# The second layer's inner weight sums and output additions of one batch: from GpSimd to VectorE

## The chip, the cores and the metric

The kernel runs on one core of one Trainium2 chip. The metric is the time of one execution on the device in microseconds (us), and where several executions are given, their median. Of the kernel before there are three: 904.57, 904.01 and 902.47 us, median 904.01. One more execution, of 905.66 us, was recorded by the hardware profiler, and all durations below come from that one. The engines are called PE (TensorE, the matmuls; PEld is its loading of weights), DVE (VectorE), ACT (ScalarE), POOL (GpSimd) and SP (SyncE, which here issues nearly all DMAs).

## The reference

Four batches of 768 tokens go through an attention block in which a query sees only the keys of its own cluster, and then through a feed-forward block of two layers. Only the latter matters here:

```python
def _moe_ref(x, w_in, w_out) -> np.ndarray:
    h = x @ w_in                                   # (3072, 512) @ (512, 2048)
    g = h * (1.0 / (1.0 + np.exp(-1.702 * h)))
    return (g @ w_out).astype(np.float32)          # (3072, 2048) @ (2048, 512)
```

## The kernel before, in words

After all the attention, the kernel runs the two layers for one batch after the other (the loop `for b in range(B)`, line 992). Both layers save matmuls by a scheme of Strassen's kind: a product of 2 x 2 blocks is made with seven block products instead of eight, and pays for it with additions of blocks before and after. The first layer (`first7`, line 843) does so once, in eight steps of seven products. The second layer does so twice, one level inside the other: seven outer products (the loop `for k in range(7)`, line 1044, in the order `ORDER = (1, 2, 3, 6, 5, 7, 4)`, line 751; called k = 0 to 6 here), and each of them is made by `second49` (line 886) from seven inner products.

Around these 49 products there are four kinds of additions, and the question is who makes them:

- The inner sums of the activations (`sums_t`, line 818): for each k four sums of 128x768, here called t3, t2, t1 and t4 in the order in which they are made, t2 and t1 depending on the one before. VectorE makes them one set ahead: during set k it makes those of k+1, two at the first, one at the second and one at the third call of `extra` in `second49`. The inner products 6, 5, 7 and 4 need t2, t1, t3 and t4. TensorE takes the products in the order 1, 2, 6, 5, 7, 3, 4, so t2 is needed first.
- The inner sums of the weights (three of 128x512, s2, s1 and s4, written by `keep_w`, line 770): the same for all batches. They are made once, in the first batch, and stored to DRAM (`kept_w`); later batches load them (`load_sums`, line 786). Those of k = 0 to 4 are made by GpSimd during the first batch's first layer, those of k = 5 and 6 during its second layer, right into the tile `Wz` from which TensorE reads them. The pool of `Wz` has two buffers, so the tile of k+2 takes that of k, and the call stands after `second49(k)`, that is after sets k = 3 and k = 4.
- The additions of an inner product into its block: 128x192, of a PSUM bank and an SBUF tile (`add`, line 841), by VectorE; y11, y12 and y22 are three quarters of the block `y`. Copies out of PSUM are ScalarE's. There are six PSUM banks, and a set takes three, so each bank comes round again two sets later.
- The additions of the finished block `y` into the output's quarters `Y[11]` to `Y[22]`, 128x768 each, at the end of `second49`: for k = 3, 4 and 5 (products 6, 5 and 7 of `ORDER`) two of them. GpSimd makes them, but in the last batch VectorE makes those of k = 4 and 5.

While VectorE is at k = 5 and 6 it also makes the sums of the next batch's x (`sums_x`, line 623, eight operations of 128x384), which the next first layer needs from its second product on; they and others are handed out by `extra`, which calls `more`. Each engine runs its instructions strictly in the order in which the program issues them. On every engine this order is the one written in the code, so an operation that is put on VectorE stands in line in front of everything that the code issues to VectorE after it. All element-wise sums go through one helper, `sums`, so line 594 stands for all of them in the profile and they are told apart by tile and shape.

Of the kernel before, what the change touches and what calls it, by code (L numbers as in the profile page):

```python
# [38 lines left out]
def fast(  # L39
# [26 lines left out]
    nc = tc.nc  # L66

    B, H, S, D = q.shape
# [523 lines left out]
    def sums(engine, todo):  # L592
        for o, a, op, b in todo:
            engine.tensor_tensor(out=o, in0=a, in1=b, op=(  # L594
                ALU.add if op == "+" else ALU.subtract))
# [157 lines left out]
    def W_of(i):  # L753

        def w(row, col):
            return lambda fq, m: w_out[
                :, row * FB + fq * FQ:row * FB + (fq + 1) * FQ,
                col * DN + m * P:col * DN + (m + 1) * P]

        def z(n):  # L760
            return lambda fq, m: Z_of[n][:, fq * FQ:(fq + 1) * FQ,
                                         m * P:(m + 1) * P]
        return {1: w(0, 0), 2: w(1, 0), 3: z(4), 4: w(1, 1), 5: z(1),
                6: z(2), 7: w(0, 1)}[i]
# [2 lines left out]
        a = W_of(i)  # L767
        sums(nc.vector, ((a(0, 1), a(0, 0), "-", a(0, 1)),))

    def keep_w(k, o):  # L770

        a = W_of(ORDER[k])
        s2, s1, s4 = o
        for i, (o, x, op, z) in enumerate((
                (s2, a(1, 1), "-", a(0, 1)), (s1, s2, "+", a(0, 0)),
                (s4, a(1, 0), "-", s2))):
            sums(nc.gpsimd, ((o, x, op, z),))
            nc.sync.dma_start(out=kept_w[k, i], in_=o)

    def spare_y():  # L780
# [3 lines left out]
    W = {}  # L784

    def load_sums(k, made=False):
        W[k] = ws.tile([P, 3, FQ, P], FP32, name="Wz")
        if made:
            keep_w(k, [W[k][:, i] for i in range(3)])
            return  # L790
        for i in range(3):
            nc.sync.dma_start(out=W[k][:, i], in_=kept_w[k, i])

    def G_of(i):

        k, h = {1: (0, 0), 7: (0, 1), 3: (1, 1), 2: (1, 0), 6: (0, 0),
                5: (1, 1), 4: (1, 0)}[i]
        return lambda fq, q: G[:, k * FB + fq * FQ:k * FB + (fq + 1) * FQ, h,
                               q * QT:(q + 1) * QT]
# [7 lines left out]
    def temps(k):  # L807

        return dict(zip((3, 2, 1, 4), (
            (tile_y(11), E[0], E[1], E[2]),  # L810
            (tile_y(12), tile_x(2), tile_x(3), tile_x(4)),
            (tile_y(21), E[0], E[1], E[2]),
            (tile_x(2), tile_x(3), tile_x(4), E[0]),
            (G_of(5)(0, 1), E[1], E[2], E[0]),
            (G_of(7)(0, 1), tile_x(3), E[1], E[2]),
            (G_of(4)(0, 1), E[0], E[1], E[2]))[k]))
# [23 lines left out]
    def add(o, p, a):  # L840
        nc.vector.tensor_tensor(out=o, in0=p, in1=a, op=ALU.add)  # L841
# [44 lines left out]
    def second49(k, extra, last):  # L886

        i = ORDER[k]
        a, g, t, w = W_of(i), G_of(i), temps(k), W.pop(k)
        A = {1: a(0, 0), 2: a(1, 0), 3: w[:, 2], 4: a(1, 1), 5: w[:, 1],  # L890
             6: w[:, 0], 7: a(0, 1)}
        M = {1: g(0, 0), 2: g(1, 0), 3: g(1, 1), 4: t[4], 5: t[1], 6: t[2],
             7: t[3]}

        def bank_b():
            return ps_b.tile([P, 512], FP32, name="b")[:, 0:QT]

        def product(ps, n, start):
            for f in range(FQ):
                nc.tensor.matmul(out=ps, lhsT=A[n][:, f], rhs=M[n][:, f],  # L900
                                 start=start and f == 0,
                                 stop=(f == FQ - 1), skip_group_check=True)

        y = Y[22] if i == 1 else ep.tile([P, 2, HALF], FP32, name="y")
        y11, y12, y21, y22 = (y[:, m, q * QT:(q + 1) * QT]
                              for m in range(2) for q in range(2))
        p5 = ep.tile([P, QT], FP32, name="p5")
        x = bank_b()
        product(x, 1, True)
        nc.scalar.copy(y11, x)  # L910
        z = bank_b()
        product(z, 2, True)
        add(y11, z, y11)
        extra(0)
        product(x, 6, False)
        nc.scalar.copy(y12, x)
        v = bank_b()
        product(v, 5, True)
        nc.scalar.copy(p5, v)
        product(x, 7, False)  # L920
        nc.scalar.copy(y22, x)
        add(y22, y22, p5)
        extra(1)
        product(v, 3, False)
        add(y12, v, y12)
        if i == 4:
            c = Y[21]
            add(c[:, 0], y[:, 0], c[:, 0])
            add(c[:, 1, QT:], y22, c[:, 1, QT:])
            extra(2)  # L930
        product(x, 4, False)
        if i == 4:
            add(c[:, 1, 0:QT], x, c[:, 1, 0:QT])
            return
        nc.scalar.copy(y21, x)
        extra(2)
        pool = nc.vector if last and i in (5, 7) else nc.gpsimd
        sums(pool, {1: (),
                    2: ((Y[11], y, "+", Y[22]),),
                    3: ((Y[12], y, "+", Y[22]),),  # L940
                    6: ((Y[12], y, "+", Y[12]), (Y[21], y, "+", Y[22])),
                    5: ((Y[12], y, "+", Y[12]), (Y[22], y, "+", Y[21])),
                    7: ((Y[22], y, "+", Y[22]), (Y[21], y, "+", Y[21]))}[i])
# [42 lines left out]
    def do(steps, n):  # L986
        for _ in range(n):
            next(steps, None)
# [3 lines left out]
    for b in range(B):  # L992
        for f in range(FB):
            first7(b, f, *XT)
            sums_w(b * FB + f + 2)
            if f:
                after7(f - 1)
            do(pend, 1)
            if b == 0 and f < 3:
                for n in range(3 * f, min(3 * f + 3, FB)):  # L1000
                    sums_z((nc.gpsimd, nc.vector, nc.vector)[n % 3], n)
            if b == 0 and f in (3, 4):
                for i in ORDER[0:4] if f == 3 else ORDER[4:]:
                    turn_w(i)
            if b == 0 and f >= 3:
                for k in {3: (0,), 4: (1, 2), 5: (3,), 6: (4,), 7: ()}[f]:
                    keep_w(k, spare_y())
                if 5 <= f < 7:
                    load_sums(f - 5)
        after7(FB - 1)  # L1010
        if b < B - 1:
            for h in range(2):
                for hp in range(HP):
                    x = xT_of[b + 1, h, hp] = xp.tile([P, HALF], FP32,
                                                      name="x")
                    nc.sync.dma_start(out=x, in_=kept[b, h, hp])
            made = sums_x(b + 1)
        else:
            made = iter(())

        def stores(b, *todo, **how):
            for n in todo:
                store(b, n, **how)
                yield

        def tail():
            store(b, 22)
            yield
            store(b, 21, q=slice(1, 2))
            store(b, 21, q=slice(0, 1), queues=(), turned=slice(0, 1))  # L1030
            yield

        def chain(*todo):
            for steps in todo:
                yield from steps

        def sums_of_x():
            for XT[:] in made:
                yield

        x_steps = sums_of_x()
        final = b == B - 1

        for k in range(7):
            nxt = sums_t(k + 1) if k < 6 else iter(())
            more = {1: sums_G(6), 2: sums_G(5), 3: sums_G(4),
                    4: stores(b, 11), 5: stores(b, 12) if final else x_steps,
                    6: tail() if final else x_steps}.get(k, iter(()))
            if b == B - 1 and k < 2:
                test(k)  # L1050
            if (b, k) == (B - 1, 6):
                is_bad = nc.values_load(bad[0:1, 0:1], min_val=0, max_val=1)

            def extra(at):
                do(nxt, (2, 1, 1)[at])
                do(more, ((1, 0, 1) if final else (0, 4, 4))[at] if k == 6
                   else (0, 0, 4)[at] if k == 2 else (0, 2, 2)[at])

            second49(k, extra, final)
            if k < 5:  # L1060
                load_sums(k + 2, b == 0 and k > 2)
            elif b < B - 1:
                load_sums(k - 5)
        pend = () if final else stores(b, 12, 22, 21)
        if final:
            store(b, 21, q=slice(0, 1), turned=slice(1, 2),
                  queues=(nc.sync, nc.scalar))
# [439 lines left out]
```

## Time and profile before

| | us |
|---|---|
| median of the three runs (lowest, highest) | 904.01 (902.47, 904.57) |
| the profiled execution | 905.66 |
| its span, first to last instruction | 903.8 |
| GpSimd's 128x512 inner weight sums in the first batch's second layer, six | 1.27 to 1.98 each |
| GpSimd's 128x768 output additions from 456 to 484 us | 2.39 each (mean of 6) |
| VectorE's 128x768 output additions in the last batch, four | 0.94 to 0.95 each |
| matmul of the second layer, 128x192 | 0.326 |

The mean granted TensorE clock is 0.995. The first batch's second layer begins at 415.27 us and the second batch's at 555.59. A time in a timeline row is the start from the beginning of the span, followed by the duration; brackets at the end of a row give the idle time before it and who ended it. VectorE's rows overlap a little at their ends, so that the distance between two starts is some 0.08 us less than a duration where the next operation doesn't need the result.

In the first batch, the sets begin on TensorE at 433.76 (k = 2), 442.86 (k = 3), 451.96 (k = 4), 461.06 (k = 5) and 471.27 (k = 6), and the next first layer at 481.59. The chain of waits that ended last goes through TensorE alone nearly everywhere; between 454.79 and 484.54 us it runs mostly over VectorE's sums. At 480.85 this chain also names a load of `Wz` that lands at 483.88, just ahead of a VectorE sum at 483.94. That sum reads x and no `Wz`, and VectorE had worked without a break until then.

### The profile page before, as it was taken

Reading aid. Unit: us, or ns where it says so; the run is one execution under the profiler, and the core shown is the slowest. Engines: PE = TensorE matmul, PEld = TensorE weight load, DVE = VectorE, ACT = ScalarE, POOL = GpSimd, SP = SyncE. Lnnn points to the kernel's source line nnn. Section 1 sums busy time; section 2 is a strip of 40 time slices with the busy share of each in tenths; the row PEclk is TensorE's granted clock in tenths of the full one; section 3 lists DMA queues with packets and bytes.
Section 4 is the critical chain, followed back from the end, with each engine's and each line's share of the span. In section 5 each row is a group of like instructions: output and inputs, shape, how many; then the busy total and the mean of one; then the engine's idle time right before and its main releaser. Section 6 shows DMA issues by size and latency. Waiting matters only on the chain.

```text
span 903.8 us, 17747 instructions
## 1 busy us (share of the span) xinstructions
PE 885.9 (98%) x6712; PEld 581.7 (64%) x6712; DVE 728.1 (81%) x1170; ACT 365.0 (40%) x816; POOL 499.2 (55%) x469
## 2 busy tenths in 40 slices
PE   8999999999999999999999999999999999999994
PEld 3444444444454445558996557997557997557994
DVE  3999989999898997998998557797556797556894
ACT  3677767776777764222111222112222112222110
POOL 5899999999999998693274211242221242220230
PEclk9999999999999999999999999999999999999998
DMA  9466556666664210036213102332102322200323
GB/s 181 113 123 116 103 119 134 139 140 137 138 134 112 85 43 18 9 127 214 70 54 122 36 1 71 105 86 83 42 1 70 106 74 90 47 1 1 105 73 71
DMA packets 177565, 78.97 MB, mean 87 GB/s; under 512 B 154440, under 2 KB 160704, under 8 KB 177472
## 3 DMA queue, kind: packets, MB, share of 16 engines
q1 hardware_dynamic: 176912, 77.63, 35.3%
q8 instruction: 55, 0.90, 0.4%
q14 instruction: 38, 0.31, 0.1%
q10 hardware_dynamic: 560, 0.13, 0.1%
HBM read 61.03 MB, written 16.70 MB: 86 GB/s over the span
## 4 chain that ended last, share of the span: by engine, by line
PE 88%; DVE 6%; issue 2%; POOL 2%; DMA 1%; SPq 0%; ACT 0%; DVEq 0%; POOLq 0%
PE b L850 32%; PE b L900 23%; PE s L468 13%; PE o L533 12%; PE m L550 3%; PE s L491 3%; DVE G L594 2%; POOL sum L517 2%; DVE E L594 1%; PE m L344 1%; DVE Tx L594 1%; DMA in<-in_k_dram 1%; DVE y L841 0%; PE o L292 0%; DMA Wz<-kept_w 0%
## 5 line engine op out<-in xcount | busy, mean ns | idle before, releaser
L517 POOL TENSOR_TENSOR sum<-sum,A 128x384 f32<-128x384 f32 x252 | 265.9, 1091 | 26.7 <-ACT A L499 16.0
L841 DVE TENSOR_TENSOR G<-b,G 128x384 f32<-128x384 f32 x224 | 123.2, 557 | 98.9 <-PE b L850 89.3
L499 ACT ACTIVATE A<-s 128x768 f32<-128x768 f32 x192 | 146.2, 808 | 91.8 <-PE s L491 73.0
L594 POOL TENSOR_TENSOR Y<-y,Y 128x768 f32<-128x768 f32 x28 | 69.2, 2487 | 174.9 <-DVE y L841 151.0
L855 ACT ACTIVATE G<-G 128x384 f32<-128x384 f32 x128 | 66.4, 523 | 199.0 <-DVE G L841 197.7
L468 PE MATMUL s<-T,T 64*64 64x384 f32 x1536 | 143.0, 487 | 0.7 <-ACT A L499 0.7
L533 PE MATMUL o<-A,inv 64*64 64x384 f32 x1536 | 141.4, 483 | 0.0
L594 POOL TENSOR_TENSOR W<-w_in 128x256 f32<-128x256 f32 x32 | 23.6, 738 | 163.8 <-PE b L850 163.5
L594 DVE TENSOR_TENSOR G<-G 128x768 f32<-128x768 f32 (+1 forms) x92 | 102.3, 1136 | 0.0
L468 PEld LDWEIGHTS s<-T,T 64*64 64x64 f32 x1536 | 55.2, 132 | 69.9 <-ACT A L499 36.4
L850 PE MATMUL b<-Tx,w_in 128*128 128x384 f32 x256 | 93.0, 486 | 0.0
L850 PE MATMUL b<-x,W 128*128 128x384 f32 x256 | 93.0, 486 | 0.0
L850 PE MATMUL b<-x,w_in 128*128 128x384 f32 x256 | 88.6, 486 | 0.0
L533 PEld LDWEIGHTS o<-A,inv 64*64 64x64 f32 x1536 | 59.1, 133 | 37.9 <-issue 32.8
L850 PEld LDWEIGHTS b<-x,W 128*128 128x128 f32 x256 | 48.6, 190 | 33.9
L850 PEld LDWEIGHTS b<-Tx,w_in 128*128 128x128 f32 x256 | 48.6, 190 | 33.9
L850 PEld LDWEIGHTS b<-x,w_in 128*128 128x128 f32 x256 | 48.5, 190 | 33.5 <-issue 0.6
L900 PE MATMUL b<-G,w_out 128*128 128x192 f32 x320 | 55.9, 326 | 0.0
L900 PEld LDWEIGHTS b<-G,w_out 128*128 128x128 f32 x320 | 52.7, 190 | 1.1
L900 PE MATMUL b<-E,Wz 128*128 128x192 f32 x288 | 51.5, 328 | 1.4 <-DVE E L594 1.4
L900 PEld LDWEIGHTS b<-E,Wz 128*128 128x128 f32 x288 | 47.1, 190 | 3.4 <-POOL Wz L594 1.3
L850 PE MATMUL b<-Tx,W 128*128 128x384 f32 x128 | 46.6, 487 | 1.5 <-DVE Tx L594 1.5
(165 smaller groups left out, 1366.9 us busy)
## 6 DMA issues: line engine op xcount, KB each, us to landing
Wz<-kept_w SPq DMA_DIRECT2D x78, 256.0 KB
raw<-in_moe_w_in_dram SPq DMA_DIRECT2D x16, 512.0 KB
raw<-in_moe_w_out_dram SPq DMA_DIRECT2D x16, 512.0 KB
inv<-in_v_dram SPq DMA_DIRECT2D x16, 384.0 KB
in<-in_q_dram SPq DMA_DIRECT2D x60, 96.0 KB
in<-in_k_dram SPq DMA_DIRECT2D x60, 96.0 KB
kept<-x SPq DMA_DIRECT2D x24, 192.0 KB
x<-kept SPq DMA_DIRECT2D x24, 192.0 KB
```

Of the source, the lines that this page charges most:

```text
L344: nc.tensor.matmul(out=ps[r:r + SQ, w * NJ * SQ:(w + 1) * NJ * SQ] .rearrange("p (j t) -> p j t", t=SQ), lhsT=cT[:, p % HP].rearrange("p a ...
L468: nc.tensor.matmul(out=ps[c:c + D, a, 0:HALF], lhsT=T[p, 1][rows, kt * P + c:kt * P + c + D], rhs=T[p, 0][rows, h * HALF:(h + 1) * HALF], ...
L491: nc.tensor.matmul(out=s_of[u][c:c + D, a, :], lhsT=rows_of[1, p % 2][rows, kt * P + c:kt * P + c + D], rhs=rows_of[0, p % 2][rows, h * HA ...
L499: nc.scalar.activation(out=A_of[u], in_=s_of.pop(u), func=AF.Exp, scale=SCALE)
L517: nc.gpsimd.tensor_tensor(out=sum_of[g][:, a], in0=(A_of[u - 1] if kt == 1 else sum_of[g])[:, a], in1=A_of[u][:, a], op=ALU.add)
L533: nc.tensor.matmul(out=o_of[g][a * D:(a + 1) * D, r, 0:HALF], lhsT=v_in[p][rows, a, kt, :], rhs=A[rows, a, :], start=(kt == 0), stop=(kt = ...
L550: nc.tensor.matmul(out=ps[a * D:(a + 1) * D, 0:HALF], lhsT=twos, rhs=sm[:, a, :], start=(i == 0), stop=(i == len(parts) - 1))
L594: engine.tensor_tensor(out=o, in0=a, in1=b, op=(ALU.add if op == "+" else ALU.subtract))
L841: nc.vector.tensor_tensor(out=o, in0=p, in1=a, op=ALU.add)
L850: nc.tensor.matmul(out=ps[:, 0:HALF], lhsT=a[:, c], rhs=x(c), start=(c == 0), stop=(c == 1))
L855: nc.scalar.activation(out=g, in_=g, func=AF.Gelu_apprx_sigmoid, scale=2.0)
L900: nc.tensor.matmul(out=ps, lhsT=A[n][:, f], rhs=M[n][:, f], start=start and f == 0, stop=(f == FQ - 1), skip_group_check=True)
```

## The change

`keep_w` gets the engine as an argument. The two sets of inner weight sums that are made in the first batch's second layer (k = 5 and k = 6, three sums each) are issued to VectorE instead of GpSimd; those made earlier stay on GpSimd. And the four output additions of k = 4 and k = 5 in the first batch are issued to VectorE, as in the last batch. In both kernels they stand at the same places in the program: the output additions at the end of `second49`, the weight sums after it.

```diff
-    def keep_w(k, o):
+    def keep_w(k, o, engine=nc.gpsimd):
 
         a = W_of(ORDER[k])
         s2, s1, s4 = o
         for i, (o, x, op, z) in enumerate((
                 (s2, a(1, 1), "-", a(0, 1)), (s1, s2, "+", a(0, 0)),
                 (s4, a(1, 0), "-", s2))):
-            sums(nc.gpsimd, ((o, x, op, z),))
+            sums(engine, ((o, x, op, z),))
             nc.sync.dma_start(out=kept_w[k, i], in_=o)
...
         W[k] = ws.tile([P, 3, FQ, P], FP32, name="Wz")
         if made:
-            keep_w(k, [W[k][:, i] for i in range(3)])
+            keep_w(k, [W[k][:, i] for i in range(3)], nc.vector)
             return
...
-            second49(k, extra, final)
+            second49(k, extra, b in (0, B - 1))
             if k < 5:
                 load_sums(k + 2, b == 0 and k > 2)
```

On VectorE this adds three `Wz` sums after set k = 3, two output additions and three `Wz` sums after set k = 4, and two output additions after set k = 5; ten instructions. GpSimd loses the same ten. The instruction lists of the other engines are the same in both kernels, with the stores of the weight sums waiting for VectorE instead of GpSimd.

## The prediction

> **What bounds the kernel now.** I read the page first, then the timeline of TensorE through the first batch's second layer beside the same stretch of the second batch, then VectorE's and GpSimd's there. The page says that TensorE is the bound of the whole:
>
> ```profile
> PE 885.9 (98%) x6712; PEld 581.7 (64%) x6712; DVE 728.1 (81%) x1170; ACT 365.0 (40%) x816; POOL 499.2 (55%) x469
> PE 88%; DVE 6%; issue 2%; POOL 2%; DMA 1%; SPq 0%; ACT 0%; DVEq 0%; POOLq 0%
> ```
>
> An edit on VectorE or GpSimd can only bring time where TensorE waits for them. Busy times of two stretches, each from the first product of a second layer to the second product of the next batch's first layer:
>
> ```profile
> 415.27:484.54 69.27, 66.36 (x398) 64.14 (x396) 63.55 (x76) 12.70 (x38) 30.13 (x14) 1.00 0.33 112
> 555.59:620.84 65.25, 65.25 (x397) 64.43 (x396) 59.23 (x79) 11.40 (x36) 19.20 (x8) 1.00 0.29 91
> ```
>
> The columns are the stretch, its length, then PE, PEld, DVE, ACT and POOL busy. The same work takes 69.27 us in the first batch and 65.25, without a gap, in the second: 4.02 us of TensorE waiting, the most that this change can give. TensorE's timeline has the waits; a product of 8 matmuls takes 1.30, one of 4 in the first layer 1.29:
>
> ```profile
> 461.06 2.76 PE L900 MATMUL b<-G,w_out 128*128 128x192 f32 x16
> 463.78 1.54 PE L900 MATMUL b<-Tx,Wz 128*128 128x192 f32 x8
> 465.99 1.54 PE L900 MATMUL b<-E,Wz 128*128 128x192 f32 x8 [0.67 <-DVE E L594]
> ...
> 471.27 2.76 PE L900 MATMUL b<-G,w_out 128*128 128x192 f32 x16
> 474.06 1.57 PE L900 MATMUL b<-E,Wz 128*128 128x192 f32 x8
> 476.32 1.54 PE L900 MATMUL b<-E,Wz 128*128 128x192 f32 x8 [0.69 <-DVE E L594]
> ...
> 484.54 1.56 PE L850 MATMUL b<-Tx,W 128*128 128x384 f32 x4 [1.49 <-DVE Tx L594]
> ```
>
> Starts against what a gapless row would give: product 6 of set k=5 is 0.12 late (463.78 for 463.66), its product 5 0.91 (465.99 for 465.08), products 6 and 5 of k=6 0.19 and 0.96, the second product of the first layer 1.66 or so; together about 4. Each waits for a VectorE sum, but for 474.06, which begins 0.05 after GpSimd's first inner weight sum of k=6 ended (472.03 + 1.98). VectorE has no idle time in this stretch, so the question is why it is late:
>
> ```profile
> 461.73 1.91 DVE L594 TENSOR_TENSOR Tx<-G 128x768 f32<-128x768 f32 x1
> 468.09 2.30 DVE L594 TENSOR_TENSOR G<-G 128x768 f32<-128x768 f32 x1
> 470.43 2.45 DVE L594 TENSOR_TENSOR E<-G 128x768 f32<-128x768 f32 x1
> 474.15 2.02 DVE L594 TENSOR_TENSOR E<-G,E 128x768 f32<-128x768 f32 x1
> 479.24 4.24 DVE L594 TENSOR_TENSOR x<-x 128x384 f32<-128x384 f32 x2
> ```
> ```profile
> 458.90 1.98 POOL L594 TENSOR_TENSOR Wz<-w_out 128x512 f32<-128x512 f32 x1
> 460.96 1.86 POOL L594 TENSOR_TENSOR Wz<-Wz,w_out 128x512 f32<-128x512 f32 x1
> 462.79 1.98 POOL L594 TENSOR_TENSOR Wz<-w_out,Wz 128x512 f32<-128x512 f32 x1
> 467.18 4.88 POOL L594 TENSOR_TENSOR Y<-y,Y 128x768 f32<-128x768 f32 x2 [2.42 <-DVE y L841]
> 478.59 4.47 POOL L594 TENSOR_TENSOR Y<-y,Y 128x768 f32<-128x768 f32 x2 [1.30 <-DVE y L841]
> ```
>
> A 128x768 sum that takes 0.95 where GpSimd idles takes 1.9 to 2.5 beside a GpSimd sum, and the two 128x384 sums at 479.24 take 4.24 instead of 1.01. GpSimd doesn't work beside VectorE here; they take turns.
>
> **What the Trainium skill says.** "SBUF — State Buffer", section "SBUF: two separate sides": a VectorE operation with two SBUF inputs and a GpSimd operation that reads SBUF hold one port pair for the whole instruction, and the other blocks. The trace agrees (0.95 against 2.45), and additions with one input in PSUM keep their 0.34 (at 467.83 and 478.11, as at 603 with GpSimd idle). "GPSIMD Engine Reference", section 3.1: a float32 tensor-tensor takes GpSimd 1.96 times VectorE's time. Here a 128x512 sum takes GpSimd 1.27 at its shortest, VectorE 0.68: 1.86 times. "Perfetto Trace Analysis", section "Optimizing Scalar/DVE Operations", warns that moving work between these two may not help because of that port; it gives no balance for the way back, which has to be counted.
>
> **The change part by part.** VectorE's costs are taken as start-to-start distances where GpSimd idles: an addition from PSUM 0.27; a 128x768 sum 0.87, or 0.97 if the next needs its result (601.21 − 600.24 in the second batch); two transposes 0.96; two 128x384 sums 0.94; the two 128x768 output additions 1.73 (877.41 to 879.14 in the last batch, where VectorE makes them already). For the inner weight sums, from the groups between 380 and 381.2 us:
>
> ```profile
> L594 DVE TENSOR_TENSOR w_out<-w_out 128x512 f32<-128x512 f32 x2 | 1.3, 684 | 0.0
> ```
>
> Two in 1.29, so the second starts 0.60 after the first; one whose result is needed next 0.71. A set of three (s2, then s1 which needs it, then s4): 0.71 + 0.60 + 0.60 = 1.91. In the trace of before no VectorE operation makes this very sum; its bounds are this 1.91 and, from VectorE's Z<-Z 128x512 beside GpSimd (1755 ns each), 5.3. I take 1.91, since after 458.94 GpSimd has nothing left in this stretch.
>
> Removed from GpSimd: six sums that held the port some 1.27 each and four output additions that held it some 1.8 (an estimate, going on from 0.73 at 128x256 and 1.27 at 128x512). Between 459.68 and 483.40 VectorE spent 23.7 us on rows that sum to 11.7 at the distances above: 12.0 lost. Added to VectorE: 2 x 1.91 + 2 x 1.73 = 7.3, in line, in front of sums that TensorE waits for. Net, VectorE is 4.7 ahead at the end; what counts is each date on the way. Walking the new order, set k by set k, from the row that ends at the unchanged 459.68 (GpSimd's two output additions of k=3 stay):
>
> The sums for k=5's weights run to 461.59; y11 to 461.86; t3 (0.97) to 462.83; t2 ends 463.78 (before: 463.64). Product 6 of k=5, wanted at 463.66, started 0.14 after t2 before, so 463.92: this wait grows from 0.12 to 0.26, the one loss. Then y22, t1 done at 464.90 for product 5 at 465.22, in time. Transposes, y12, t4 to 466.90; the two output additions to 468.63; weight sums of k=6 to 470.54; y11, t3 to 471.78; t2 ends 472.73, and with 0.14 is 0.15 ahead of product 6 of k=6 at 473.02. t1 ends 473.86 for 474.32. Two sums of x, y12, t4, two sums of x to 476.79; output additions to 478.52; y11, y22; the first half of the x sum that held TensorE at 484.54 ends at 479.60, for a product due at 480.81. So this product starts 484.54 − 480.81 = 3.73 us earlier, and from there TensorE ran without a gap to the end of the next batch's second layer, so the gain stays.
>
> Hidden parts: SyncE's queue gets the three stores of each weight set from VectorE at 461.6 and 470.5 instead of 464.8 and 477.3, so what follows them, the output stores at 466.82 and the next loads at 477.74, is not later. The additions y11 and y12, which release PSUM banks, are delayed behind the new sums, but k=4's y11 at 461.59 frees a bank wanted only at 471.7. The last addition of k=6 ends near 482.7, and its bank is wanted by the fourth first-layer product at 483.4: 0.7 of cover. The new sums' waits on old loads of the same weight tile, last issued at 441.76, have long passed.
>
> Sum against the profiled execution: span 903.8 − 3.73 = 900.1; the execution, 905.66 with 1.9 outside the span, 901.9. It lies 1.65 above the median of 904.01, so for the median: 900.3.
>
> **The rivals.** First, part of the wait comes back: with an inner weight sum dearer by d each, t2 of k=5 is 3d late and t2 of k=6 6d, and the gain is 3.73 − (6d − 0.15). At a sum every 0.95 us (d = 0.35) it is 1.8, inside what can be told from no change; for it speaks that only 0.15 covers t2 of k=6, against it that the same shape took 0.68 on w_out before. One every 0.85 gives about 901.6. Second, no change: the wait turns up behind the last one, at PSUM banks held by VectorE's additions in the first tiles of the next layer; it would take 3.7 us beyond a cover of 0.7, and VectorE would have to be 4 us later than walked; about 904. Third, slower: VectorE becomes the bound at t2 of k=6, because the six sums take their contended 1.75 us. Break-even is d = 0.65, a sum every 1.25; two Z<-Z rows took 3.44, so one every 1.69 (d = 1.09), and the loss is 6.54 − 0.15 − 3.73 = 2.66, time 906.7. For it: this time is in the trace, three times. Against it: each time a GpSimd sum ran beside it, and here none is left. That the sums stay on GpSimd is excluded, as the instruction lists of both kernels show them moved.
>
> **How the numbers follow.** The forecast 900.3, with its own 899.0 to 901.3: the ceiling of 4.02 gives 900.0, the shown runs spread by 1 us to each side of their middle, and an uncertainty of 0.1 a sum takes 0.5. Chance 0.79. The first rival 0.12, half of it still above the bound, the second 0.04, the third 0.05. A measurement of this kernel can tell about 0.2%, 1.8 us, from no change. Faster 0.79 + 0.06 = 0.85, same 0.06 + 0.04 = 0.10, slower 0.05. Range 898.9 to 902.4.
>
> **What would show it.** Right: VectorE's 128x768 sums after 460 us at 0.95; Wz sums on VectorE near 0.68; the first layer's second product near 480.8, with a wait of some 0.3 before product 6 of k=5 as the only one left. Wrong: Wz sums over 0.95, a product 6 of k=6 later than 474, or a gap in the first tiles of the next first layer.

## The result, and the profile after

| | before | after |
|---|---|---|
| median of seven runs each, us | 904.57 (902.47 to 905.15) | 901.13 (898.69 to 902.26) |
| ratio, 95% interval | | 0.996 [0.9949, 0.997] |
| span of the profiled execution, us | 903.8 | 900.4 |
| first batch's second layer to the second product of the next layer, us | 69.27 | 65.66 |

The kernel became 3.4 us faster in the medians, 0.4%. The interval lies below 1; in microseconds it is 2.7 to 4.6. The last row is the stretch that the prediction looked at, from 415.27 to 484.54 us before and from 415.48 to 481.14 after: 3.61 us shorter. What stands in front of it took 0.21 us more in this execution, so the span shows 3.61 − 0.21 = 3.40.

The page after: the busy times, and the shares of the chain that ended last.

```profile
PE 884.9 (98%) x6712; PEld 582.0 (65%) x6712; DVE 723.6 (80%) x1180; ACT 365.0 (41%) x816; POOL 477.0 (53%) x459
PE 93%; DVE 3%; POOL 2%; issue 1%; DMA 0%; SPq 0%; ACT 0%; DVEq 0%; POOLq 0%
```

VectorE makes ten instructions more and is busy 4.5 us less (723.6 against 728.1). GpSimd makes ten fewer and is busy 22.2 us less, though the ten are worth some 15 us by themselves (an estimate: six at 1.27, four at the estimated 1.8). The rest was time in which one engine waited for the other, and the profile books it as busy.

TensorE's timeline after, from the begin of set k=5:

```profile
461.29 2.76 PE L900 MATMUL b<-G,w_out 128*128 128x192 f32 x16
464.18 1.54 PE L900 MATMUL b<-Tx,Wz 128*128 128x192 f32 x8
465.55 1.46 PE L900 MATMUL b<-E,Wz 128*128 128x192 f32 x8
...
473.35 2.76 PE L900 MATMUL b<-E,Wz 128*128 128x192 f32 x16
...
481.14 1.45 PE L850 MATMUL b<-Tx,W 128*128 128x384 f32 x4
```

Product 6 of k=5 is 0.29 late (464.18, wanted at 461.29 + 2.60 = 463.89), and its first matmuls cost 0.07 more. All other waits are gone: products 6 and 5 of k=6 follow each other in one merged row from 473.35, and the next first layer runs without a gap. VectorE's timeline for the same time:

```profile
459.90 0.68 DVE L594 TENSOR_TENSOR Wz<-w_out 128x512 f32<-128x512 f32 x1
460.62 0.69 DVE L594 TENSOR_TENSOR Wz<-Wz,w_out 128x512 f32<-128x512 f32 x1
461.23 0.68 DVE L594 TENSOR_TENSOR Wz<-w_out,Wz 128x512 f32<-128x512 f32 x1
...
463.08 0.96 DVE L594 TENSOR_TENSOR Tx<-G 128x768 f32<-128x768 f32 x1
...
472.05 0.96 DVE L594 TENSOR_TENSOR E<-G 128x768 f32<-128x768 f32 x1
...
476.14 1.02 DVE L594 TENSOR_TENSOR x<-x 128x384 f32<-128x384 f32 x2
```

The 128x512 sums take 0.68 to 0.69. The sums that took 1.91, 2.45 and 4.24 before take 0.96, 0.96 and 1.02.

### The profile page after: what moved, and what is told of

It is laid out like the page before. It is cut to its first block, busy times and chain, and to the rows that moved or that the text cites. A ratio compares the mean times of both kernels' runs of the same rounds, so it can differ in the third digit from the quotient of the medians.

```text
span 900.4 us, 17736 instructions
## 1 busy us (share of the span) xinstructions
PE 884.9 (98%) x6712; PEld 582.0 (65%) x6712; DVE 723.6 (80%) x1180; ACT 365.0 (41%) x816; POOL 477.0 (53%) x459
## 4 chain that ended last, share of the span: by engine, by line
PE 93%; DVE 3%; POOL 2%; issue 1%; DMA 0%; SPq 0%; ACT 0%; DVEq 0%; POOLq 0%
PE b L850 32%; PE b L900 28%; PE s L468 13%; PE o L533 12%; PE s L491 3%; PE m L550 3%; POOL sum L517 2%; PE m L344 1%; PE o L292 0%; DVE G L841 0%; PE m L330 0%; DVE x L571 0%; PE s L482 0%; DMA short<-in_centroids_dram 0%; PE m L356 0%
## 5 line engine op out<-in xcount | busy, mean ns | idle before, releaser
L594 POOL TENSOR_TENSOR Y<-y,Y 128x768 f32<-128x768 f32 x24 | 58.1, 2434 | 171.2 <-DVE y L841 147.3
L855 ACT ACTIVATE G<-G 128x384 f32<-128x384 f32 x128 | 66.3, 523 | 197.3 <-DVE G L841 195.9
```

Source lines behind the costliest of these rows:

```text
L594: engine.tensor_tensor(out=o, in0=a, in1=b, op=(ALU.add if op == "+" else ALU.subtract))
L855: nc.scalar.activation(out=g, in_=g, func=AF.Gelu_apprx_sigmoid, scale=2.0)
```

## The experiments

The theory: VectorE's sums were late because GpSimd's sums take turns with them, and TensorE waited for VectorE. (The experiments test the taking turns; that a port of the SBUF is what is taken in turns, they don't show.) Rivals: TensorE waited for GpSimd's own results; only one of the two moves matters; VectorE's queue has slack, so that its new work costs nothing. Every kernel is measured on the stretch named above, in one profiled execution each. It is steadier than the whole time: its first part, up to the begin of set k=5, is the same work for TensorE in every kernel and took 45.79 to 45.85 us in all eleven, while seven executions of one kernel spread by about 3 us. The stretch is 69.27 before and 65.66 after, and 65.25 in the second batch, where nothing waits.

| kernel | stretch, us | whole time against the kernel before |
|---|---|---|
| weight sums alone moved | 67.32 | 0.9985 [0.9978, 0.9992] |
| output additions alone moved | 67.47 | 0.998 [0.9973, 0.9987] |
| changed, GpSimd makes six idle sums | 70.86 | 1.0027 [1.0016, 1.0039] |
| changed, GpSimd makes six memsets | 65.71 | one run |
| changed, weight sums made twice | 69.90 | 1.0013 [1.0004, 1.0022] |
| changed, k=3's additions moved too | 65.28 | 0.9959 [0.9946, 0.9973] |
| before, without the six weight sums | 65.31 | one run |
| changed, three idle sums | 69.64 | one run |
| changed, four idle sums | 70.16 | one run |

The ratios are against executions of the kernel before that were taken with each: 47 with a median of 903.31 us, and for the six idle sums 10 with a median of 903.91.

**Each part alone.** First only the weight sums moved:

```diff
-            second49(k, extra, b in (0, B - 1))
+            second49(k, extra, final)
```

> Only the six inner weight sums go to VectorE; the four output additions stay on GpSimd. Measured on the stretch from the first second-layer product of the first batch to the second product of the next first layer (69.27 us before, 65.66 after the whole change). Turn-taking theory: VectorE is as in the second batch (where GpSimd also makes the four additions) plus two times 1.91; t2 of k=5 is then 0.3 late, t2 of k=6 about 1 more, the x sums 0.4 more: stretch 66.7 to 67.3, that is 2.0 to 2.6 us won. Rival (TensorE waited for GpSimd's own late weight sums, and the output additions are no matter): with the weight sums off GpSimd the whole gain is there, stretch 65.7.

The stretch is 67.32, 0.02 above the first range and far from the rival's 65.7. TensorE's and VectorE's timelines of this kernel:

```profile
473.10 2.84 PE L900 MATMUL b<-E,Wz 128*128 128x192 f32 x16 [1.02 <-DVE E L594]
481.38 1.56 PE L850 MATMUL b<-Tx,W 128*128 128x384 f32 x4 [0.25 <-DVE Tx L594]
```
```profile
465.70 2.30 DVE L594 TENSOR_TENSOR Wz<-w_out 128x512 f32<-128x512 f32 x1
468.04 2.19 DVE L594 TENSOR_TENSOR Wz<-Wz,w_out 128x512 f32<-128x512 f32 x1
470.15 0.68 DVE L594 TENSOR_TENSOR Wz<-w_out,Wz 128x512 f32<-128x512 f32 x1
```

The moved weight sums of k=6 now run into the output additions that GpSimd still makes: two of the three take 2.30 and 2.19 for 0.68, and t2 behind them holds TensorE for 1 us. So the second move also protects the first.

Then only the output additions moved, with the weight sums left on GpSimd (`keep_w` as before).

> Only the four output additions go to VectorE; the six weight sums stay on GpSimd, which now makes those of k=6 right behind those of k=5, since nothing stands between them in its queue. Turn-taking theory: VectorE's sums between 459 and 468 us still double, t2 of k=5 is as late as before (0.1), t1 of k=5 0.9 or more late, but from about 470 on VectorE's sums take 0.95 and the waits of k=6 and of the next first layer shrink: stretch 67.0 to 68.2, 1.1 to 2.3 us won. Rival (late weight sums from GpSimd): the sums of k=6 are now ready by 469 and of k=5 as before, so only waits of k=5 are left, stretch 66.3.

The stretch is 67.47. The one long wait of TensorE in this kernel, and VectorE's row behind it:

```profile
465.45 1.54 PE L900 MATMUL b<-E,Wz 128*128 128x192 f32 x8 [1.74 <-DVE E L594]
```
```profile
463.29 2.02 DVE L594 TENSOR_TENSOR E<-G,Tx 128x768 f32<-128x768 f32 x1
```

But for 0.13 us at product 6 of k=5, all the rest, k=6 and the next layer, runs without a wait, as the theory has it; the rival's number, 66.3, is missed. Alone, the parts bring 1.95 and 1.80 us; their sum, 3.75, is close to the 3.61 of both.

**Taking turns by itself.** Into the changed kernel go six GpSimd sums whose result nobody reads:

```diff
+    spare = sp.tile([P, FQ, 96], FP32, name="spare")
...
             keep_w(k, [W[k][:, i] for i in range(3)], nc.vector)
+            w = W_of(ORDER[k])
+            for _ in range(3):
+                sums(nc.gpsimd, ((spare, w(1, 1)[:, :, 0:96], "-",
+                                  w(0, 1)[:, :, 0:96]),))
             return
```

> The changed kernel, and GpSimd makes six further 128x384 sums of w_out into a spare tile that nobody reads, issued where the weight sums stood before. No result of GpSimd is waited for any more. Turn-taking theory: VectorE's operations with two SBUF inputs between 459 and 468 us lose 0.7 to 1.0 each to them, some 4.5 in all, t2 of k=5 is 3.5 to 4 late and t2 of k=6 pulls the stretch to 69.0 to 71, so that the gain of the change is gone. Rival (the waits came from results of GpSimd that were late): nothing waits for these sums, VectorE keeps its 0.95, stretch 65.7.

The gain is gone, and more: 70.86. GpSimd's timeline, then VectorE's, then TensorE's:

```profile
457.45 9.26 POOL L594 TENSOR_TENSOR spare<-w_out 128x384 f32<-128x384 f32 x6
```
```profile
458.23 1.48 DVE L594 TENSOR_TENSOR Wz<-w_out 128x512 f32<-128x512 f32 x1
459.75 1.37 DVE L594 TENSOR_TENSOR Wz<-Wz,w_out 128x512 f32<-128x512 f32 x1
461.04 1.48 DVE L594 TENSOR_TENSOR Wz<-w_out,Wz 128x512 f32<-128x512 f32 x1
462.45 0.34 DVE L846 TENSOR_TENSOR y<-b,y 128x192 f32<-128x192 f32 x1
```
```profile
466.00 2.67 PE L905 MATMUL b<-Tx,Wz 128*128 128x192 f32 x8 [3.63 <-DVE Tx L594]
468.47 2.06 PE L905 MATMUL b<-E,Wz 128*128 128x192 f32 x8
```

From the first weight sum to t1 VectorE needs 8.62 us (458.23 to 466.85) instead of 4.32 after the change (459.90 to 464.22): 4.30 lost to six sums, 0.72 each. An operation with one input in PSUM between them keeps its 0.34. Nothing waits for these sums, so what VectorE lost here can't come from late results of GpSimd. In the kernel before, the one wait that ended with a GpSimd sum is that of 0.19 us at 474.06. But the way was not quite the expected one: all six fell in front of k=5, the matmuls after the long wait were slow and cost 1.76 us (more on that below), and k=6 had no wait. The slow matmuls hid one: at full speed product 6 of k=6 would have been wanted at 475.10 and not at 476.86, and its t2 ended at 475.64.

The same with memsets in their place (`nc.gpsimd.memset(spare, 0.0)`), which write SBUF and read nothing:

> As the six idle sums, but GpSimd writes zeros into the spare tile (memset, 128x384), so that it writes SBUF without reading it. If only a GpSimd operation that reads SBUF takes turns with VectorE: VectorE's sums stay at 0.95 and the stretch at 65.6 to 65.8. If every GpSimd operation does: VectorE's sums beside them lose the memset's duration each, and the stretch is over 66.5.

```profile
457.68 2.81 POOL L792 MEMSET spare<- 128x384 f32 x6
```
```profile
459.19 0.69 DVE L594 TENSOR_TENSOR Wz<-Wz,w_out 128x512 f32<-128x512 f32 x1
```

VectorE's sum beside them takes 0.69, and the stretch is 65.71. The Trainium skill says so too ("SBUF — State Buffer", section "SBUF: two separate sides"): only a GpSimd operation that reads SBUF blocks a VectorE operation with two SBUF inputs.

**The price in VectorE's queue.** Each weight sum on VectorE is issued twice:

```diff
-            sums(engine, ((o, x, op, z),))
+            for _ in range(2 if engine is nc.vector else 1):
+                sums(engine, ((o, x, op, z),))
```

> The changed kernel with each of the six weight sums on VectorE made twice, into the same place with the same values; this doubles the cost that the change put in front of t2. Turn-taking theory with VectorE's queue as the price: a set gets 1.8 to 2.1 dearer, t2 of k=5 is late by that much more, t2 of k=6 by twice as much, and the stretch grows by twice the extra less the cover: 65.66 + 3.5 to 3.9 = 69.2 to 69.6, about what it was before the change. Rival (there is slack behind t2 of k=5, or TensorE's waits have another cause): one set's extra at most, 65.7 to 67.7.

```profile
464.21 1.54 PE L901 MATMUL b<-Tx,Wz 128*128 128x192 f32 x8 [2.31 <-DVE Tx L594]
...
475.37 2.84 PE L901 MATMUL b<-E,Wz 128*128 128x192 f32 x16 [1.82 <-DVE E L594]
```

A set now takes 4.10 us (457.76 to 461.86 on VectorE) for 1.93, so 2.17 more, a little over what was assumed, and the stretch, 69.90, is 0.3 above its range. It grows by 4.24: product 6 starts 2.18 later at k=5, another 1.98 later at k=6 (2.17 less a cover of 0.19), and the first matmuls after that wait cost 0.08. The prediction's sum, 6d less 0.15, gives 4.19. The whole time is above that of the kernel before. VectorE's queue has no slack here beyond these 0.19; the move pays because a weight sum costs 0.64 there (1.93 for three).

**The last wait.** The two output additions of k=3 are moved too, in the first batch alone:

```diff
-            second49(k, extra, b in (0, B - 1))
+            second49(k, extra, (5, 6, 7) if b == 0 else
+                     (5, 7) if final else ())
...
-        pool = nc.vector if last and i in (5, 7) else nc.gpsimd
+        pool = nc.vector if i in last else nc.gpsimd
```

> The changed kernel with the two output additions of k=3 of the first batch on VectorE as well, so that GpSimd has nothing to do beside VectorE from k=3 on. Turn-taking theory: the two sums of G after 454.9 take 0.95 each and not 5.05 together, so VectorE starts the first weight sum near 458.6 and not 459.9, t2 of k=5 is in time, and the last wait of 0.29 before product 6 of k=5 goes: stretch 65.3 to 65.4, 0.3 us below the change, which is under what the whole time can tell. Rival (VectorE's two more operations in line delay t2 as the weight sums did): that wait grows to 0.5 or more and the stretch to 66 or more.

```profile
458.20 2.77 PE L900 MATMUL b<-G,w_out 128*128 128x192 f32 x16
460.80 1.47 PE L900 MATMUL b<-Tx,Wz 128*128 128x192 f32 x8
```

Product 6 of k=5 follows at 2.60 without a wait, and the stretch is 65.28, 0.03 over that of the second batch. By the trace this beats the changed kernel by 0.38 us. The whole time can't tell the two: 0.9959 [0.9946, 0.9973] against 0.996 [0.9949, 0.997]. Its profiled span, 896.5, is not evidence: its second layer began 3 us earlier than in the changed kernel's execution, in a part that both have in common.

**The ceiling.** The kernel before, with sets k=5 and k=6 taking stored sums of other sets instead of making their own:

```diff
-        if made:
-            keep_w(k, [W[k][:, i] for i in range(3)])
-            return
         for i in range(3):
-            nc.sync.dma_start(out=W[k][:, i], in_=kept_w[k, i])
+            nc.sync.dma_start(out=W[k][:, i],
+                              in_=kept_w[k if k < 5 else k - 2, i])
```

> The kernel before, without the six weight sums of k=5 and k=6: these sets take the stored sums of k=3 and k=4 in every batch, so the output is not the reference's. The output additions stay on GpSimd. Turn-taking theory: the first batch's second layer is then that of the second batch, stretch 65.2 to 65.4, the ceiling of 4.0 us, though GpSimd still makes all output additions. Rival (the output additions on GpSimd alone already make TensorE wait): stretch over 66.

The stretch is 65.31. So GpSimd's output additions alone hold nothing up: VectorE's lead bears them. It doesn't bear GpSimd's weight sums, not even with the output additions of k=4 and 5 taken off GpSimd (67.47 above). And once the weight sums stand in VectorE's own queue, GpSimd's output additions cost TensorE time too (67.32 above).

**The slow matmuls.** In the kernel with six idle sums TensorE's matmuls were slow for a while after the wait. Two kernels with fewer sums were to tell whether this belongs to the wait. One keeps only the three that are issued with the weight sums of k=5, the other these and one of those of k=6:

> The changed kernel with only the first three of the six idle GpSimd sums. With six, VectorE lost 0.72 a sum, but TensorE also lost 1.8 us in slow matmuls (514 and 416 ns for 326) after one wait of 3.8 us. If that slowness belongs to the length of the wait, half as many sums delay t2 of k=5 by 0.81 + 0.69 + 0.81 = 2.3, TensorE waits 2.6 there, all matmuls keep 326 ns but for the first, and the stretch is 65.66 + 2.3 = 67.9 to 68.1. If it belongs to the idle sums (reads of w_out beside TensorE's weight loads, say), half of it stays: 68.7 to 69.

> The same with four idle sums: t2 of k=5 is another 0.5 later, TensorE waits some 3.1 at once. Without slow matmuls the stretch is 68.4 to 68.7; with them, as after the wait of 3.8, over 69.5.

Both expectations for three sums fail: the stretch is 69.64. With four it is 70.16, above the 69.5 that stood for slow matmuls. The loss against 1.30 a product is the same each time: three sums (464.70 to 469.06) 4.36 − 2.60 = 1.76; four (465.64 to 471.29) 5.65 − 3.90 = 1.75; six (466.00 to 470.36) 4.36 − 2.60 = 1.76. So the number of sums doesn't matter. Without this loss three and four sums give 67.88 and 68.41, as the queue's arithmetic had them.

What it is can be read from the busy times by stretch. The first number after the length is PE busy, the third from the right the granted clock. With three and with four sums:

```profile
461.77:465.18 3.41, 1.00 (x7) 0.73 (x6) 3.38 (x6) 0.00 (x0) 0.11 (x1) 1.00 0.41 154
465.18:468.60 3.42, 3.42 (x13) 3.42 (x12) 3.42 (x7) 0.32 (x1) 0.00 (x0) 0.50 0.21 46
```
```profile
463.60:467.01 3.41, 1.37 (x8) 1.40 (x9) 3.38 (x5) 0.00 (x0) 0.08 (x1) 1.00 0.20 77
467.01:470.43 3.42, 3.42 (x13) 3.42 (x12) 3.42 (x7) 0.64 (x2) 0.00 (x0) 0.50 0.42 91
```

The clock is halved for 3.41 us and then full again; half of that, 1.71, is lost. With four sums eight matmuls run at full speed first, and the slow time comes 1.4 us after the wait. With each weight sum made twice, the longest wait was 2.47 us (461.74 to 464.21), and the clock stayed full. In the kernel before it falls at the very end, where TensorE has run out of work and GpSimd does nothing. Here are the doubled sums, then the end of the kernel before:

```profile
462.41:465.82 3.41, 1.61 (x10) 1.64 (x11) 3.38 (x6) 0.03 (x1) 0.00 (x0) 1.00 0.20 77
465.82:469.24 3.42, 3.42 (x23) 3.42 (x22) 3.42 (x6) 0.93 (x3) 0.00 (x0) 1.00 0.48 104
```
```profile
891.52:894.94 3.42, 0.70 (x5) 0.41 (x3) 2.09 (x7) 0.00 (x0) 0.00 (x0) 1.00 0.22 49
894.94:898.35 3.41, 0.00 (x0) 0.00 (x0) 0.00 (x0) 0.00 (x0) 0.00 (x0) 0.50 0.18 37
```

In every trace the changes of the clock lie whole multiples of 3.413 us apart: with three sums it is full again at 468.60 and falls next at 895.26, 125 such lengths later. So each trace divides into windows of this length. In the eleven traces 14 windows at full clock had TensorE busy for 40% or less (with six, three and four sums 7%, 29% and 40%), and half clock followed each of them; it followed none of the 2834 with 47% or more. So what goes with the fall is how little TensorE does in one window, and not the idle sums. The wait of 2.57 us with three sums lay in one window; the wait of 2.47 lay across two, which were busy for 85% and 47%.

## Why the prediction was right

Point by point, with the median's shift forecast at 3.73 and measured at 3.44 us, and the stretch 3.61 shorter:

- The ceiling of 4.02 us in TensorE's waits stands: without the weight sums the stretch came to 65.31, 3.96 less than before.
- The cause, VectorE and GpSimd taking turns, is shown by the idle sums: no consumer, and VectorE loses 0.72 to each. Of the two places given for additions with one input in PSUM, the one at 478.11 shows nothing, since GpSimd was idle from 477.29 to 478.59. The one at 467.83 does, and so does the one between the idle sums.
- The late starts before add up to 3.84, not to 4.02. Most of the rest is that the products behind the waits of 0.67 and 0.69 us took 0.08 and 0.07 longer than 1.30 (465.99 to 467.37, 476.32 to 477.69), a term that the walk left out.
- The price of a set of weight sums was taken as 1.91 and is 1.93; the two output additions, taken as 1.73, are 1.74 (467.14 to 468.88).
- The one loss, product 6 of k=5, was put at 0.26 and is 0.29. The thin cover at t2 of k=6, put at 0.15 and 0.19 by the doubled sums, held: t2 ended at 473.01 and the product began at 473.35 on time.
- The second product of the next layer was forecast 65.54 after the start of the layer and came after 65.66. Of the missing 0.12, 0.03 is the wait and 0.07 the slower matmuls just after it.
- The level was 0.8 us off (901.13 for 900.3), 0.56 of it because the kernel before measured 904.57 over seven runs and not 904.01. That the median's shift comes within 0.3 of the forecast is partly luck: its interval is 2.7 to 4.6. The stretch is the better witness.
- The rival of a partly returning wait stayed away, since the sums were as cheap as in the row it was judged by. The second rival's wait at PSUM banks didn't come: TensorE runs through the first tiles of the next layer without a gap. The rival of a slower kernel was right in its arithmetic: doubled sums, 1.37 each (4.10 for three), cross the break-even of 1.25, and the kernel was slower. What it left out is the clock: where a wait empties enough of one window, 1.76 us come on top of its length, so beyond the break-even the loss can be larger than a sum of waits shows.

## What to carry to other kernels

Where two engines take turns, count an operation twice: at its own duration on the one engine, and at what it takes from the other's queue. Here each idle GpSimd sum of 128x384 took 0.72 us from VectorE's queue, while VectorE makes a larger sum, 128x512, in 0.64. So handing such sums to GpSimd was worth nothing as soon as VectorE set the pace. Compare the stretch with a twin that lacks the load, here the second batch: its difference is the ceiling of what a remedy for these waits can give, and the walk from one due date to the next says how much of it a certain remedy gets.

## What was not expected of the hardware

After waits of TensorE of 2.57, 3.1 and 3.8 us the granted clock fell to 0.50 for 3.41 us, 0.3 to 1.4 us after the end of the wait, and each time 1.75 to 1.76 us were lost. After a wait of 2.47 us it did not fall. The Trainium skill ("TensorE: Matmul & The Clock Gate", section "Part 1: The HAM clock gate (the "warmup" mystery)") has half the clock after an idle window of about 3.4 us. The half and the length agree with the traces. But the window need not be empty: half clock followed one in which TensorE was busy for 40%, and it did not follow those with 47%. Where between the two the border lies is not shown. A wait's place against these windows therefore counts as well as its length, and a sum of waits alone doesn't show this cost.
